# The last head's values ahead of the fourth modulation in a decode block: the order of one load and of the matmuls behind it

## The chip, the cores and the metric

The kernel runs on one core of a Trainium2 chip. The metric is the device time of one execution in microseconds (us); the median of three runs stands for a kernel. The profile is of one execution of its own, and its times are counted from the start of its span.

## What is computed

A transformer block in decode: two sequences (B = 2), one new token each, model width 512, 32 heads of width 128 over 4096 cached positions, everything in 32-bit floats. Conditioning vectors `c` give six modulations (shift, scale and gate of each half). Cut to its core, the reference is:

```
mod = silu(c) @ w_mod                    # [2, 6 * 512] -> sa, ca, ga, sb, cb, gb  (modulations 0 to 5)
h = layernorm(x) * (1 + ca) + sa
q = h @ wq                               # 32 heads x 128
p = softmax(q . k_cache * 128**-0.5)     # over 4096 positions, per head
x = x + ga * ((p @ v_cache) @ wo)        # ga: modulation 2
h = layernorm(x) * (1 + cb) + sb         # cb: modulation 4, sb: modulation 3
h = h @ w1 + b1                          # 512 -> 1376
x = x + gb * ((h * tanh(softplus(h))) @ w2)   # gb: modulation 5
```

The two caches alone are 268 MB, and each value of them is used once.

## The kernel before, in words

**Loads.** The host lays all inputs out beforehand as one stream of rows of 128 partitions. `stream()` (lines 40 to 75) lists 36 loads in order. Most fill one buffer of 64 KB a partition; there are three such buffers (tile name `room`), so load n can be issued only when the readers of load n-3 in the same place are done (`used`, line 167). `load` (line 146) issues a load's transfers from SyncE (SP), line 163, in the order of the list. In the trace all of them are "room<-in_load", L163.

The last four loads (lines 66 to 74) matter here. Load 32 has the values of head 28, the last two pieces of `wo` and modulation 2. Load 33 has the values of heads 29 and 30. Load 34 (line 69) has the weights of modulation 4 (`m4`, 1024 KB) and the values of head 31, in two parts of 2048 KB (`("v", 31, 0)` and `("v", 31, 1)`); it goes as a transfer of 3072 KB (`m4` and part 0) and two of 1024 KB (the halves of part 1). Behind them in the same load stands `m5p`, a part of modulation 5's weights that uses only 24 rows. It goes in eight small transfers over rows named in `DEAL` (line 18): three of one row, two of three rows, three of five rows, 8 KB a row. `EARLY = 4` (line 17) says how many of the eight are issued ahead of the load's large transfers; the rest come behind them (lines 160 to 163). Load 35 has modulation 3 with half of `w1` (2400 KB), the other half (1376 KB), then the rest of modulation 5 with the first chunk of `w2` (1024 KB), and the other ten chunks of `w2` in four transfers (1280, 768, 256 and 256 KB).

**Heads.** For each head, VectorE multiplies the keys by the query (line 342) and sums (line 345), 8.7 us each; this runs beside the stream. TensorE (PE) weights the values (`weighted_v`, line 379, matmul at line 385) into a PSUM bank.

**Tail.** The order of all instructions is written out by hand. From line 484 on, PE does: values of heads 29 and 30 with a stretch of `busy` dummies between; `head_values` and `project_o` for them; part 0 of head 31's values (line 521); `fold_att` (line 522, matmul at 516), which folds the attention output of the other heads; part 1 of head 31's values (line 523), in the middle of which, through the argument `idle`, stand three quarters of modulation 4 (`modulation`, matmul at line 271). Then the sums of head 31 are copied out (line 524), turned (line 526, matmul at 408) and projected (`head_out_q`, line 528, matmul at 424); the last quarter of modulation 4 follows (line 529), two dummies, and two terms of modulation 5 (line 548, matmul at 543). VectorE makes the new x (lines 552 and 555); `centred` (line 224) takes its mean and variance by two small matmuls (lines 234 and 242), and what stands in its argument `between` is issued to PE in the middle: here three dummies (line 559). Then come modulation 3 (line 560), two more terms of modulation 5, the first feed-forward matmul (line 577), the activation, the rest of modulation 5, the second feed-forward matmul over eleven chunks of `w2` (line 622), and two VectorE operations (629, 630) before the store.

`busy(n)` (line 318, matmul at 322) issues matmuls whose result nobody reads, one instruction of the program for up to two blocks of 128 columns. A 32-bit matmul shows as two instructions in the trace, so `busy(3)` is four of them and `modulation` over three quarters is 24.

Of the kernel before, what the change touches and what calls it, by code (L numbers as in the profile page):

```python
# [9 lines left out]
AF = mybir.ActivationFunctionType  # L10
# [3 lines left out]
P = 128  # L14
WIDTHS = (384, 384, 352, 256)
CHUNKS = [(g, j) for j in range(3) for g in range(4) if WIDTHS[g] > P * j]
EARLY = 4
DEAL = [slice(j, j + 1) for j in (33, 34, 35)] + [slice(32, 41, 4), slice(3, 12, 4)] + [slice(j, 20, 4) for j in range(3)]
PLACES = sorted(p for deal in DEAL for p in range(deal.start, deal.stop, deal.step or 1))
BLOCK = 44  # L20
# [1 line left out]
WHOLE = len(PIECES)  # L22
# [6 lines left out]
W = 2048  # L29
HALF = BIG // 2  # L30
# [9 lines left out]
def stream():  # L40


    order, n_v = [], 0
    for h in range(1, HEADS):
        order.append(("k", h))
        if h % HC == HC - 1 and HC < h < HEADS - 1:
            c = (h + 1) // HC
            order.append([("wq", c), ("wo", c - 2)])
        if h not in AHEAD:
            order += [("v", n_v, 0), ("v", n_v, 1)]  # L50
            n_v += 1
    order = [x if isinstance(x, list) else [x] for x in order]

    def size(x):
        return sum(SIZES[key[0]] for key in x)

    loads = [[([("m01", 0), ("wq", 0), ("wq", 1)], (4 * W,)), ([("k", 0)], (BIG,))]]
    for _ in range(1, HEADS):
        row = []
        while size(row) < ROW:  # L60
            room = ROW - size(row)
            row += order.pop(next(i for i, x in enumerate(order) if size(x) <= room))
        loads.append([(row, (ROW,))])
    last = [("v", h, i) for h in range(HEADS - 4, HEADS) for i in range(2)]
    assert order == [[key] for key in last[:2]], order
    loads += [
        [(last[:2] + [("wo", 6), ("wo", 7), ("m2", 0)], (BIG + 3 * W,))],
        [(last[2:4], (BIG,)), (last[4:6], (BIG,))],
        [([("m4", 0)] + last[6:], (W + HALF, W, W)), ([("m5p", 0)], (512 * WHOLE,))],
        [  # L70
            ([("m3", 0), ("w1", 0)], (W + 2 * sum(WIDTHS), 2 * sum(WIDTHS))),
            ([("m5", 0), ("w2", 0)], (512 * (M5 + 1), 5 * 512, 3 * 512, 512, 512)),
        ],
    ]
    return loads
# [3 lines left out]
def kernel(  # L79
# [17 lines left out]
    nc = tc.nc  # L97
# [7 lines left out]
    H = HEADS  # L105
# [13 lines left out]
    def small_ps(name):  # L119
        return psum.tile([P, 512], F32, tag="sm", name=name, bufs=2)  # L120

    def wide_ps(name):
        return psum.tile([P, 512], F32, tag="mm", name=name, bufs=2)
# [19 lines left out]
    w_t = {}  # L143
    done = set()

    def load(n):
# [3 lines left out]
        for keys, srcs in loads[n]:  # L150
            take(t[:, lo:], keys)
            for src in srcs:
# [5 lines left out]
                else:  # L158
                    nc.gpsimd.memset(dst, 0.0)  # L159
                    deals = [(dst[deal], src[deal]) for deal in DEAL]  # L160
                    early, parts = deals[:EARLY], parts + deals[EARLY:]
        for dst, src in early + parts:
# [4 lines left out]
    def used(*keys):  # L167

        nonlocal loaded
        done.update(keys)  # L170
        while loaded < len(loads) and (
            loaded < 3 or all(key in done for keys, _ in loads[loaded - 3] for key in keys)
        ):
            load(loaded)
            loaded += 1
# [8 lines left out]
    bias = const.tile([P, NJ * G + NP5 * B], F32, name="bias")  # L184
    nc.scalar.dma_start(out=bias, in_=b1c)
    c5 = bias[:, NJ * G :]
    bias = bias[:, : NJ * G]
# [36 lines left out]
    def centred(src, name, first_sum=None, between=None):  # L224

        rs = const.tile([P, 8], F32, name=f"rs_{name}")
        xc = work.tile([P, P], F32, tag="xc", name=f"xc_{name}", bufs=1)
        sq = work.tile([P, P], F32, tag="sq", name=f"sq_{name}", bufs=1)
        if first_sum is None:
            nc.vector.tensor_reduce(out=rs[:, 0:1], in_=src, axis=AX.X, op=ALU.add)  # L230
        else:
            first_sum(rs[:, 0:1])
        mps = small_ps(f"mean_{name}")
        nc.tensor.matmul(mps[:, 0:1], lhsT=mean_w, rhs=rs[:, 0:1], start=True, stop=True)
        nc.vector.tensor_scalar(out=xc, in0=src, scalar1=mps[:, 0:1], scalar2=None, op0=ALU.subtract)
        nc.vector.scalar_tensor_tensor(
            sq, xc, 1.0, xc, op0=ALU.mult, op1=ALU.mult, accum_out=rs[:, 1:2]
        )
        if between is not None:
            between()  # L240
        vps = small_ps(f"var_{name}")
        nc.tensor.matmul(vps[:, 0:1], lhsT=mean_w, rhs=rs[:, 1:2], start=True, stop=True)
        return xc, vps[:, 0:1], rs
# [20 lines left out]
    def modulation(name, n, t, ps=None, ks=range(G)):  # L264


        if ps is None:
            ps = wide_ps(f"modps{name}")[:, : n * P].rearrange("p (m n) -> p m n", m=n)
        for k in ks:
            for g in range(G):  # L270
                nc.tensor.matmul(  # L271
                    ps[R * g : R * (g + 1)],
                    lhsT=ct[:, k, :],
                    rhs=t[:, k, :].rearrange("p (m n) -> p m n", m=n)[:, :, P * g : P * (g + 1)],
                    start=(k == 0),
                    stop=(k == G - 1),
                )
        return ps
# [9 lines left out]
    xc, var, rs = centred(xq, "a")  # L288
# [29 lines left out]
    def busy(n, bank=1):  # L318

        for lo in range(0, n, 2):  # L320
            cols = P * min(2, n - lo)
            nc.tensor.matmul(ov[bank][:, :cols], lhsT=ident, rhs=e_t[0].rearrange("p c m -> p (c m)")[:, :cols], start=True, stop=True)  # L322


    NB = NS // 4
# [50 lines left out]
            out=t[:, :4, :], in0=own, in1=t[:, 4:5, :].to_broadcast([P, 4, B * HC]), op=ALU.mult,  # L376
        )

    def weighted_v(h, part, bank, first=True, last=True, idle={}):

        for c in range(NB // 2):
            if c in idle:
                idle[c]()
            g = c % G
            nc.tensor.matmul(  # L385
                ov[bank][R * g : R * (g + 1), :],
                lhsT=e_t[h % HC][:, NB // 2 * part + c, :],
                rhs=v_t[h, part][:, c, :],
                start=(first and part == 0 and c < G),
                stop=(last and part == 1 and c >= NB // 2 - G),  # L390
            )
        used(("v", h, part))

    def value_sums(bank, copies):

        o_t.clear()
        n = 4 // len(copies)
        for i, copy in enumerate(copies):
            o = work.tile([P, 4, DH], F32, tag="o", name=f"o{bank}")[:, :n]
            copy(o.rearrange("p m d -> p (m d)"), ov[bank][:, n * DH * i : n * DH * (i + 1)])  # L400
            for m in range(n):
                o_t[n * i + m] = o[:, m, :]
# [18 lines left out]
    def head_out_q(h):  # L421

        for g in range(G):
            nc.tensor.matmul(
                xps[R * g : R * (g + 1), :P],
                lhsT=ot_t[h // HC % 2][:, h % HC, :],
                rhs=wo_t[h // HC][:, h % HC, P * g : P * (g + 1)],
                start=False, stop=(h == H - 1), skip_group_check=True,
            )
# [54 lines left out]
    N = H // HC - 1  # L484
# [13 lines left out]
    for h in range(H - 3, H - 1):  # L498
        if h == H - 2:
            busy(24, 1 - N % 2)  # L500
        for part in range(2):
            weighted_v(h, part, N % 2, False, h == H - 2)
# [8 lines left out]
    mps4 = wide_ps("modps4")[:, :P].rearrange("p (m n) -> p m n", m=1)  # L511

    def fold_att():

        for g in range(G):
            nc.tensor.matmul(
                xps[R * g : R * (g + 1), :P], lhsT=fold, rhs=att_sb[:, P * g : P * (g + 1)],
                start=True, stop=False, skip_group_check=True,
            )

    weighted_v(H - 1, 0, 1 - N % 2)
    fold_att()
    weighted_v(H - 1, 1, 1 - N % 2, idle={NB // 4: lambda: modulation("4", 1, w_t["m4"], mps4, (0, 1, 2))})
    value_sums(1 - N % 2, (nc.scalar.copy, nc.vector.tensor_copy))
    busy(3)
    head_values(N, HC - 1, HC)
    busy(2)
    head_out_q(H - 1)
    modulation("4", 1, w_t["m4"], mps4, (3,))
    busy(2)  # L530
    wm3, wm5 = w_t["m3"], w_t["m5"]
    w1_t, w2_t = w_t["w1"], w_t["w2"]
    gps = ov[1 - N % 2][:, :P]
# [5 lines left out]
    def modulation_5(lo, hi):  # L539
        for n in range(lo, hi):  # L540
            c, w = terms5[n]
            for g in range(G):
                nc.tensor.matmul(  # L543
                    gps[R * g : R * (g + 1)], lhsT=c, rhs=w[:, P * g : P * (g + 1)],
                    start=(n == 0), stop=(n == len(terms5) - 1),
                )

    modulation_5(0, 2)

    xg = work.tile([P, P], F32, tag="sq", name="xg", bufs=1)  # L550
    x2 = const.tile([P, P], F32, name="x2")
    nc.vector.tensor_tensor(out=xg, in0=xps[:, :P], in1=mod[2], op=ALU.mult)
# [2 lines left out]
        nc.vector.scalar_tensor_tensor(x2, xg, 1.0, xq, op0=ALU.mult, op1=ALU.add, accum_out=total)  # L555

    m4 = work.tile([P, P], F32, tag="xn", name="m4", bufs=1)
    nc.scalar.activation(m4, mps4[:, 0, :], AF.Copy, bias=1.0)
    xc, var, rs = centred(x2, "b", add_x, lambda: busy(3))
    mps3 = modulation("3", 1, wm3)  # L560
    busy(1)
    modulation_5(2, 4)
# [156 lines left out]
```

## Time and profile before

| what | us |
|---|---|
| median of 3 runs (lowest, highest) | 694.71 (694.52, 694.92) |
| the profiled execution's own time | 694.6 |
| its span | 693.2 |
| VectorE busy, share of the span | 587.9, 85% |
| PE busy | 289.9, 42% |
| data moved, mean rate | 297.48 MB, 429 GB/s |

The span runs from the first to the last instruction of the program; 1.4 us of the execution's own time lie around it. In a row of the timeline stand the start, the time from the first start to the last end, engine, line, operation, tiles (out<-in), shapes and count, and in brackets how long the engine had been idle and what ended that. PE is a matmul, PEld the weight load ahead of it. In a row of the table by stretches stand the stretch, its length, each engine's busy time with its instructions, the clock granted to PE (1.00 is full), the busy share of the sixteen DMA engines (it can pass 1 by rounding at the edges) and GB/s.

### The profile page before, as it was taken

Reading aid. Unit: us, or ns where it says so; the run is one execution under the profiler, and the core shown is the slowest. Engines: PE = TensorE matmul, PEld = TensorE weight load, DVE = VectorE, ACT = ScalarE, POOL = GpSimd, SP = SyncE. Lnnn points to the kernel's source line nnn. Section 1 sums busy time; section 2 is a strip of 40 time slices with the busy share of each in tenths; the row PEclk is TensorE's granted clock in tenths of the full one; section 3 lists DMA queues with packets and bytes.
Section 4 is the critical chain, followed back from the end, with each engine's and each line's share of the span. In section 5 each row is a group of like instructions: output and inputs, shape, how many; then the busy total and the mean of one; then the engine's idle time right before and its main releaser. Section 6 shows DMA issues by size and latency. Waiting matters only on the chain.

```text
span 693.2 us, 4056 instructions
## 1 busy us (share of the span) xinstructions
PE 289.9 (42%) x1698; PEld 109.5 (16%) x1698; DVE 587.9 (85%) x223; ACT 44.2 (6%) x169; POOL 6.3 (1%) x21
## 2 busy tenths in 40 slices
PE   3403334335145524335242716245334425134898
PEld 1201001001012201101100301011101111001355
DVE  2799899999999999999999999999999999899202
ACT  1000000000000000000000000000000010000011
POOL 2000000000000000000000000000000000000100
PEclk9855666668565566556585565656575657656799
DMA  9999999999999999999999999999999999999997
GB/s 381 467 424 424 425 424 469 429 427 431 424 425 465 428 427 436 424 431 451 427 427 442 425 450 431 427 428 442 424 446 429 424 446 432 427 439 419 423 429 318
DMA packets 6994, 297.48 MB, mean 429 GB/s; under 512 B 928, under 2 KB 1064, under 8 KB 1448
## 3 DMA queue, kind: packets, MB, share of 16 engines
q1 hardware_dynamic: 6672, 297.14, 99.2%
q8 instruction: 13, 0.21, 0.1%
q10 hardware_dynamic: 304, 0.09, 0.1%
q14 instruction: 5, 0.04, 0.0%
HBM read 297.16 MB, written 0.07 MB: 429 GB/s over the span
## 4 chain that ended last, share of the span: by engine, by line
DMA 68%; DVE 28%; PE 4%; issue 0%; ACT 0%; SPq 0%; DVEq 0%; ACTq 0%
DMA room<-in_load 68%; DVE room L342 14%; DVE s L345 14%; PE modps L271 1%; PE ov L322 1%; PE qps L315 1%; PE w1ps L577 0%; PE yps L622 0%; PE ov L543 0%; PE ov L385 0%; PE fps L592 0%; PE otp L408 0%; DVE m L358 0%; DVE hcw L304 0%; ACT q L316 0%
## 5 line engine op out<-in xcount | busy, mean ns | idle before, releaser
L342 DVE TENSOR_TENSOR room<-room,q 128x8192 f32<-128x8192 f32 x32 | 278.2, 8693 | 45.3 <-DMA room<-in_load 40.9
L345 DVE TENSOR_REDUCE s<-room 128x64 f32<-128x8192 f32 x32 | 277.9, 8684 | 0.4 <-DVE m L358 0.3
L385 PE MATMUL ov<-room,e 128*32 128x512 f32 x1024 | 174.0, 834 | 73.1 <-ACT e L361 63.2
L354 PE MATMUL mt<-d,same 128*128 128x64 f32 x64 | 18.6, 385 | 196.4 <-DVE d L352 196.4
L385 PEld LDWEIGHTS ov<-room,e 128*32 128x32 f32 x1024 | 39.0, 145 | 177.6 <-issue 130.7
L361 ACT ACTIVATE e<-s,m 64x64 f32<-64x64 f32 x64 | 22.1, 345 | 554.2 <-DVE m L358 553.4
L354 PEld LDWEIGHTS mt<-d,same 128*128 128x128 f32 x64 | 13.4, 262 | 226.4 <-DVE d L352 180.9
L315 PE MATMUL qps<-room,hcw 128*128 128x512 f32 x64 | 42.0, 819 | 4.2 <-DMA room<-in_load 3.5
L369 PE MATMUL l<-l,ones 128*128 128x8 f32 x16 | 4.6, 359 | 74.9 <-ACT e L361 74.9
L408 PE MATMUL otp<-pick,o 128*128 128x8 f32 (+2 forms) x72 | 14.3, 326 | 34.5 <-ACT o L400 32.6
L315 PEld LDWEIGHTS qps<-room,hcw 128*128 128x128 f32 x64 | 16.4, 268 | 25.1 <-issue 19.7
L408 PEld LDWEIGHTS otp<-pick,o 128*128 128x128 f32 x72 | 13.6, 282 | 42.6 <-ACT o L400 39.8
L400 DVE COPY o<-ov 128x256 f32<-128x256 f32 x1 | 0.4, 425 | 22.9 <-ACT o L400 22.9
L369 PEld LDWEIGHTS l<-l,ones 128*128 128x128 f32 x16 | 3.8, 297 | 76.3 <-ACT e L361 76.3
L416 PE MATMUL att<-room,ot 128*32 128x512 f32 x62 | 10.2, 718 | 5.2 <-DMA room<-in_load 4.6
L361 ACT ACTIVATION_READ_ACCUMULATOR e<-s,m 64x1 f32 x64 | 11.8, 184 | 0.0
L322 PE MATMUL ov<-e,ident 128*128 128x256 f32 (+1 forms) x46 | 11.4, 380 | 0.0
L358 DVE TENSOR_REDUCE m<-mt 128x1 f32<-128x64 f32 x32 | 7.0, 218 | 5.1 <-PE mt L354 5.1
L352 DVE TENSOR_SCALAR d<-half,m 128x64 f32<-128x64 f32 x32 | 9.6, 299 | 1.1
L322 PEld LDWEIGHTS ov<-e,ident 128*128 128x128 f32 x46 | 8.0, 190 | 3.8 <-issue 3.1
L350 DVE TENSOR_REDUCE m<-s 128x1 f32<-128x64 f32 x32 | 7.0, 218 | 0.9
L159 POOL MEMSET room<- 44x2048 f32 x1 | 1.8, 1804 | 637.2 <-DVE s L345 637.2
(108 smaller groups left out, 71.4 us busy)
## 6 DMA issues: line engine op xcount, KB each, us to landing
room<-in_load SPq DMA_DIRECT2D x4, 4096.0 KB, 25.0
room<-in_load SPq DMA_DIRECT2D x1, 7168.0 KB, 38.9
room<-in_load SPq DMA_DIRECT2D x1, 3072.0 KB, 22.4
room<-in_load SPq DMA_DIRECT2D x3, 1024.0 KB, 22.0
room<-in_load SPq DMA_DIRECT2D x1, 2400.0 KB
room<-in_load SPq DMA_DIRECT2D x1, 1376.0 KB, 14.0
room<-in_load SPq DMA_DIRECT2D x1, 1280.0 KB, 14.4
room<-in_load SPq DMA_DIRECT2D x1, 768.0 KB
```

The costliest lines, as they stand in the source:

```text
L315: nc.tensor.matmul(ps, lhsT=hcw[:, k, :], rhs=wq_t[ch][:, k, :], start=(k == 0), stop=(k == G - 1))
L322: nc.tensor.matmul(ov[bank][:, :cols], lhsT=ident, rhs=e_t[0].rearrange("p c m -> p (c m)")[:, :cols], start=True, stop=True)
L342: nc.vector.tensor_tensor(out=k_t[h], in0=k_t[h], in1=qv, op=ALU.mult)
L345: nc.vector.tensor_reduce(out=s_t[h], in_=k_t[h], axis=AX.X, op=ALU.add)
L350: nc.vector.tensor_reduce(out=m_t[h][:, 0:1], in_=s_t[h], axis=AX.X, op=ALU.max)
L352: nc.vector.tensor_scalar(out=d, in0=half, scalar1=m_t[h][:, 0:1], scalar2=None, op0=ALU.mult)
L354: nc.tensor.matmul(mps[h], lhsT=same, rhs=d, start=True, stop=True)
L361: nc.scalar.activation(e_t[i][own_b, :, M * i + 4 * b : M * i + 4 * b + 4], s_t[h][own_b].rearrange("p (c m) -> p c m", m=4), AF.Exp, bias ...
L369: nc.tensor.matmul(lps[n], lhsT=ones, rhs=sum_t[n % 2], start=True, stop=True)
L385: nc.tensor.matmul(ov[bank][R * g : R * (g + 1), :], lhsT=e_t[h % HC][:, NB // 2 * part + c, :], rhs=v_t[h, part][:, c, :], start=(first a ...
L408: nc.tensor.matmul(tps[:, x], lhsT=o_t[m], rhs=pick_t[n][:, m, x], start=(m == 0), stop=(m == 3),)
L416: nc.tensor.matmul(att[R * i : R * (i + 1), :], lhsT=ot_t[n % 2][:, i, :], rhs=wo_t[n][:, i, :], start=(n == 0), stop=(n == H // HC - (2 i ...
```

## The change

In load 34 the values of head 31 stand first and modulation 4 behind them: the transfers are now 2048 KB (part 0), 1024 and 1024 KB (part 1) and 1024 KB (`m4`), one more than before. Five of the eight small transfers of `m5p` go ahead instead of four, the fifth being one of three rows. On PE, three quarters of modulation 4 move from the middle of head 31's values to behind `head_out_q`. Its last quarter, the copy of its result on ScalarE, and the first two terms of modulation 5 move into the middle of `centred`, in place of the three dummies; two more dummies are gone. The argument `idle` goes, as nothing uses it.

```diff
@@ -14,7 +14,7 @@
 P = 128
 WIDTHS = (384, 384, 352, 256)
 CHUNKS = [(g, j) for j in range(3) for g in range(4) if WIDTHS[g] > P * j]
-EARLY = 4
+EARLY = 5
 DEAL = [slice(j, j + 1) for j in (33, 34, 35)] + [slice(32, 41, 4), slice(3, 12, 4)] + [slice(j, 20, 4) for j in range(3)]
 PLACES = sorted(p for deal in DEAL for p in range(deal.start, deal.stop, deal.step or 1))
 BLOCK = 44
@@ -66,7 +66,7 @@
     loads += [
         [(last[:2] + [("wo", 6), ("wo", 7), ("m2", 0)], (BIG + 3 * W,))],
         [(last[2:4], (BIG,)), (last[4:6], (BIG,))],
-        [([("m4", 0)] + last[6:], (W + HALF, W, W)), ([("m5p", 0)], (512 * WHOLE,))],
+        [(last[6:] + [("m4", 0)], (HALF, W, W, W)), ([("m5p", 0)], (512 * WHOLE,))],
         [
             ([("m3", 0), ("w1", 0)], (W + 2 * sum(WIDTHS), 2 * sum(WIDTHS))),
             ([("m5", 0), ("w2", 0)], (512 * (M5 + 1), 5 * 512, 3 * 512, 512, 512)),
@@ -376,11 +376,9 @@
             out=t[:, :4, :], in0=own, in1=t[:, 4:5, :].to_broadcast([P, 4, B * HC]), op=ALU.mult,
         )
 
-    def weighted_v(h, part, bank, first=True, last=True, idle={}):
+    def weighted_v(h, part, bank, first=True, last=True):
 
         for c in range(NB // 2):
-            if c in idle:
-                idle[c]()
             g = c % G
             nc.tensor.matmul(
                 ov[bank][R * g : R * (g + 1), :],
@@ -520,14 +518,13 @@
 
     weighted_v(H - 1, 0, 1 - N % 2)
     fold_att()
-    weighted_v(H - 1, 1, 1 - N % 2, idle={NB // 4: lambda: modulation("4", 1, w_t["m4"], mps4, (0, 1, 2))})
+    weighted_v(H - 1, 1, 1 - N % 2)
     value_sums(1 - N % 2, (nc.scalar.copy, nc.vector.tensor_copy))
     busy(3)
     head_values(N, HC - 1, HC)
     busy(2)
     head_out_q(H - 1)
-    modulation("4", 1, w_t["m4"], mps4, (3,))
-    busy(2)
+    modulation("4", 1, w_t["m4"], mps4, (0, 1, 2))
     wm3, wm5 = w_t["m3"], w_t["m5"]
     w1_t, w2_t = w_t["w1"], w_t["w2"]
     gps = ov[1 - N % 2][:, :P]
@@ -545,8 +542,6 @@
                     start=(n == 0), stop=(n == len(terms5) - 1),
                 )
 
-    modulation_5(0, 2)
-
     xg = work.tile([P, P], F32, tag="sq", name="xg", bufs=1)
     x2 = const.tile([P, P], F32, name="x2")
     nc.vector.tensor_tensor(out=xg, in0=xps[:, :P], in1=mod[2], op=ALU.mult)
@@ -555,8 +550,14 @@
         nc.vector.scalar_tensor_tensor(x2, xg, 1.0, xq, op0=ALU.mult, op1=ALU.add, accum_out=total)
 
     m4 = work.tile([P, P], F32, tag="xn", name="m4", bufs=1)
-    nc.scalar.activation(m4, mps4[:, 0, :], AF.Copy, bias=1.0)
-    xc, var, rs = centred(x2, "b", add_x, lambda: busy(3))
+
+    def between():
+
+        modulation("4", 1, w_t["m4"], mps4, (3,))
+        nc.scalar.activation(m4, mps4[:, 0, :], AF.Copy, bias=1.0)
+        modulation_5(0, 2)
+
+    xc, var, rs = centred(x2, "b", add_x, between)
     mps3 = modulation("3", 1, wm3)
     busy(1)
     modulation_5(2, 4)
```

## Prediction

> **What bounds the kernel now.** I read the page first, then the table by stretches for the end of the stream, then the timeline of the last 30 us, then the issues of the late loads.
>
> ```profile
> span 693.2 us, 4056 instructions
> q1 hardware_dynamic: 6672, 297.14, 99.2%
> ```
>
> The load queue kept the sixteen DMA engines busy for 99.2% of the span: the kernel lasts as long as its stream, plus what is left after it. How much is left, by stretches of the end:
>
> ```profile
> 674.00:684.00 10.00, 9.95 (x136) 7.49 (x139) 2.86 (x13) 1.68 (x6) 0.42 (x1) 1.00 0.99 418
> 684.00:687.00 3.00, 2.44 (x40) 1.62 (x36) 0.18 (x1) 0.78 (x4) 0.00 (x0) 1.00 1.00 419
> 687.00:688.00 1.00, 1.00 (x25) 0.52 (x14) 0.84 (x5) 0.03 (x1) 0.00 (x0) 1.00 0.82 334
> 688.00:689.00 1.00, 1.00 (x30) 0.75 (x32) 0.29 (x2) 0.00 (x0) 0.00 (x0) 1.00 0.69 270
> 689.00:690.00 1.00, 1.00 (x46) 1.00 (x40) 0.00 (x0) 0.00 (x0) 0.00 (x0) 1.00 0.47 162
> 690.00:691.00 1.00, 0.87 (x32) 0.58 (x24) 0.07 (x1) 0.00 (x0) 0.00 (x0) 1.00 0.00 0
> ```
>
> The last number but one is the DMA share: full to 687, then some engines run dry, and the last bytes move at about 690.0. That is late: the second feed-forward matmul, which ends the kernel, has been running since 688.25. So two ends are close together, the stream's and that of the tail's own chain. The timeline of the tail shows the second:
>
> ```profile
> 667.84 1.25 PEld L385 LDWEIGHTS ov<-room,e 128*32 128x32 f32 x16 [0.47 <-DMA room<-in_load]
> 669.60 0.61 PE L516 MATMUL xps<-att_sb,fold 128*32 128x128 f32 x8
> 670.26 0.16 PEld L385 LDWEIGHTS ov<-room,e 128*32 128x32 f32 x8 [0.32 <-DMA room<-in_load]
> 671.15 0.84 PE L271 MATMUL modps<-room,ct 128*32 128x128 f32 x24
> 672.88 0.16 PEld L385 LDWEIGHTS ov<-room,e 128*32 128x32 f32 x8 [1.16 <-DMA room<-in_load]
> 673.88 0.92 PE L322 MATMUL ov<-e,ident 128*128 128x256 f32 x4
> 676.05 0.43 PE L424 MATMUL xps<-room,ot 128*32 128x128 f32 x8
> 676.30 0.40 PE L271 MATMUL modps<-room,ct 128*32 128x128 f32 x8
> 676.63 0.70 PE L322 MATMUL ov<-e,ident 128*128 128x256 f32 x2
> 677.09 0.08 DVE L555 DVE_READ_ACCUMULATOR x<-xg,cx 128x1 f32 x1
> 677.26 0.64 PE L543 MATMUL ov<-room,ct 44*32 44x128 f32 x16
> 677.83 0.38 PE L234 MATMUL mean_b<-rs_b,mean_w 128*128 128x1 f32 x2
> 678.07 0.90 PE L322 MATMUL ov<-e,ident 128*128 128x256 f32 x4
> 678.79 0.08 DVE L236 DVE_READ_ACCUMULATOR sq_b<-xc_b 128x1 f32 x1
> 679.02 0.35 PE L242 MATMUL var_b<-rs_b,mean_w 128*128 128x1 f32 x2
> 679.31 1.08 PE L271 MATMUL modps<-room,ct 128*32 128x128 f32 x32
> 682.38 2.77 PE L577 MATMUL w1ps<-room,h2t 128*32 128x384 f32 x32
> 688.25 2.61 PE L622 MATMUL yps<-room,actt 96*32 96x128 f32 x88
> 690.93 0.29 DVE L629 TENSOR_TENSOR y<-yps,mod 128x128 f32<-128x128 f32 x1 [2.64 <-PE yps L622]
> ```
>
> Three times PE waits for head 31's values: the transfer of 3072 KB is there at 667.84, the next two of 1024 KB at 670.26 and 672.88. From there to 690.93 the chain of waits names no DMA.
>
> **The change part by part.** The landing times of all that follows are needed. Two issues of load 35 show theirs, the second half of `w1` and the five chunks of `w2`:
>
> ```profile
> L163 SPq DMA_DIRECT2D room<-in_load x1: 328/328/328, 667.8 to 667.8; - x1
> DMA to landing us min/median/max: 14.0/14.0/14.0
> ...
> L163 SPq DMA_DIRECT2D room<-in_load x1: 328/328/328, 672.9 to 672.9; - x1
> DMA to landing us min/median/max: 14.4/14.4/14.4
> ```
>
> So the second half of `w1` is complete at 667.8 + 14.0 = 681.8 and the five chunks at 672.9 + 14.4 = 687.3. The pace in between is that of the slowest engines: 670.26 - 667.84 = 2.42 us for 1024 KB. Between 672.84 and 681.8 lie 2400 + 1376 KB, 9.0 us, the same pace. Modulation 3 with the first half of `w1` therefore lands at about 672.84 + 9.0 x 2400/3776 = 678.5. After 687.3 come 768, 256 and 256 KB, at that pace 1.8, 0.6 and 0.6 us: landings at about 689.1, 689.7 and 690.3. These are estimates, and the last agrees with bytes that move until 690.0.
>
> *Order of the load.* The bytes stay the same. Part 0 now comes 1024 KB earlier (667.84 - 2.42 = 665.4), the last quarter of the values takes the middle slot (670.26), and `m4` the last (672.88). The fifth early transfer puts at most three rows of 8 KB (24 KB) ahead of the values; spread over its engines that is one row each, 8/64 of a 1024 KB transfer's share of an engine (64 KB), 2.42/8 = 0.3 us, and only if it hit a slowest engine. All from load 35 on keeps its place in the stream.
>
> *One transfer more, in SP's queue.* A late issue of load 35 comes at the landing of an earlier transfer (672.9 against the landing that PE saw at 672.88; 667.8 against 667.84), so issues are held by earlier landings. With one transfer more, and smaller ones, these come no later than before. A late issue would be covered by the 14 us of stream queued ahead of it; with that cover gone each microsecond would move the end. The stream itself pays for the cut of rows of 24 KB into 16 and 8 KB. Bounds: nothing, as 3072 + 1024 KB in long rows should do no better than the 2.42 us per 1024 KB seen for 8 KB rows; and 0.2 us, as the second such transfer took 672.88 - 670.26 = 2.62. A gain is excluded, since no bytes go. I take 0.05, nearer the first pair. The Trainium skill ("DMA: Bandwidth & Descriptors", Anatomy of one DMA) gives each transfer a fixed 2.0 us besides its bytes, on the GpSimd path; by that a queued transfer more would cost 2.0. The measured 2.42 us for a whole queued transfer speaks against it here.
>
> *PE up to the projection.* Part 0 of head 31 no longer waits, and starts at 667.84 or up to 0.2 before, when the work ahead of it ends. From its start to the fold are 669.60 - 667.84 = 1.76 us, the fold takes about 0.4 (0.66 to the next start less most of the 0.32 waited), part 1 another 1.76, with no wait since its last quarter is there at 670.26. The dummies then start at 671.8 instead of 673.88: 2.1 earlier, not 2.6, since PE's work is now the limit. The projection (676.05) moves to 674.0.
>
> *Modulation 4 and the dummies.* Three quarters of it, 24 matmuls of 0.84 us together, lay in the wait for the values and now stand behind the projection. There they run while VectorE makes x (676.05 to 677.17, 1.1 us), which covers them; with no cover they would cost 0.84. `m4` is there at 672.9, 1.1 before. What they replace was longer: last quarter 0.33 (676.30 to 676.63), dummies 0.63, modulation 5 0.57, which held the mean's matmul until 677.83 though x was summed at 677.17. The mean now starts at about 675.1, 2.7 earlier. In the middle of the mean and the variance, 0.33 + 0.57 = 0.9 of real work replaces three dummies of about 0.9. The variance comes at about 676.25, 2.8 earlier.
>
> *What is late next.* Modulation 3's matmuls could start at 676.5, and their weights land at 678.5. So 2.0 of the 2.8 us turn into a wait, with the rest of PE's queue behind it: this stage starts 0.8 before its old 679.31. The same 0.8 carries to the second feed-forward matmul, at 687.5. It takes (2.61 - 0.27)/87 x 8 = 0.215 us a chunk (0.27 is the drain of one matmul). Chunk 6 is wanted at 687.5 + 6 x 0.215 = 688.8 and lands at 689.1; the last chunk is then wanted at 690.0 and lands at 690.3. Before, it was wanted at 688.25 + 10 x 0.215 = 690.4. So the end moves by -0.1 for the wait that ends last, +0.05 for the cut rows: about nothing. On the profiled execution's 694.6 that is 694.55; the median stands 0.1 above it, at 694.71, so I say 694.6 for the median. Of 2.8 us made in the middle all are lost again to the weights behind.
>
> **The rivals.** *The stream does not bind at the end* (faster). If the estimated landings were wrong and all 2.8 us reached the end, the time would be 691.9. For it: the chain of waits names PE, not DMA, after 672.88. Against it: bytes move until 690.0, so the last chunk can't be worked on before; even with landings at the last bytes the gain is 0.4. Chance 0.02.
>
> *The clock falls in the new wait* (slower). PE idles from 676.6 to 678.5, where the dummies kept it busy. Earlier in the trace such gaps set the clock of the next 3.41 us:
>
> ```profile
> 586.85:590.27 3.42, 1.43 (x16) 0.22 (x8) 3.42 (x1) 0.00 (x0) 0.00 (x0) 1.00 1.04 446
> 590.27:593.68 3.41, 0.00 (x0) 0.00 (x0) 3.41 (x3) 0.14 (x1) 0.00 (x0) 1.00 0.97 423
> 648.29:651.71 3.42, 1.64 (x16) 0.88 (x16) 1.11 (x6) 1.35 (x6) 0.00 (x0) 1.00 0.99 419
> 651.71:655.12 3.41, 3.41 (x20) 0.85 (x16) 0.00 (x0) 0.00 (x0) 0.00 (x0) 0.50 0.92 396
> ```
>
> A stretch with PE busy 1.64 of 3.42 (0.48) was followed by the half clock, one with 1.43 (0.42) was not: somewhere under a half it decides. A stretch that holds the whole gap of 1.9 has 1.5 busy (0.44), one that cuts the gap has more. A half clock for 3.41 us loses up to 1.7 of PE work, less the 0.8 in hand: the end 0.9 later, 695.5, still within 0.2%. Two such stretches lose 3.4, less 0.8: 697.2, slower. For the second, the half-clock stretch would have to be idle too; modulation 3 and `w1` fill it, and a full one (651.71) went back to 1.00 at once. Chance of one 0.15, of two 0.04. The Trainium skill ("TensorE: Matmul & The Clock Gate", Part 1) drops the clock only after about 3.4 us of idling; by that this gap costs nothing and the time is the forecast's. The stretch of 0.48 shows that less can do.
>
> *A transfer more is paid in the stream* (slower). The upper bound is what a whole transfer of 1024 KB takes, 2.42 us: 697.0; it decides once the price passes 1.4 us. Against it the pace above, where one follows on the other with nothing between. Chance 0.02. By the fixed time in the Trainium skill ("DMA: Bandwidth & Descriptors", Anatomy of one DMA) it would be 696.6.
>
> **How the numbers follow.** Forecast (nothing reaches the end) 0.77, clock once 0.15, clock twice 0.04, a paid transfer 0.02, a free tail 0.02. A measurement of this kernel tells about 0.2%, 1.4 us, from no change. Faster 0.02; slower 0.06; the same 0.92. The range takes the forecast with the last bytes' 0.4 below, 694.3, to the one fall of the clock, 695.6.
>
> **What would show it.** In the changed profile: head 31's three value groups at L385 without a DMA wait, the dummies after them at about 671.8; the projection (L424) at 674.0, the mean (L234) at 675.1; a wait of about 2 us for a load ahead of L271 x32, which starts at 678.5; the start of L622 at 687.5 with its 88 matmuls stretched to about 3.2 us; the last bytes at 690.0 as before, y (L629) within 0.2 of 690.93. The forecast is wrong if the DMA share falls to zero well before or after 690.0, or if the granted clock shows 0.5 after 676.

## The result and the profile after

| kernel | median us (lowest, highest, executions) | span of the profiled execution |
|---|---|---|
| before | 694.80 (694.52, 695.17, 6) | 693.2 |
| after | 698.38 (697.50, 698.94, 6) | 696.8 |

The ratio is 1.005, with a 95% interval of 1.004 to 1.006: slower by 3.6 us, where no change was forecast. First the page of the changed kernel, its span and its load queue:

```profile
span 696.8 us, 4044 instructions
q1 hardware_dynamic: 6816, 297.14, 98.7%
```

The stream did not become longer: 98.7% of 696.8 is 687.7 us of packets, and of before 99.2% of 693.2 was 687.7. Nor does it end later. By stretches (the last number but two is the clock granted to PE, the last but one the DMA share):

```profile
688.00:689.00 1.00, 0.81 (x9) 0.11 (x2) 0.00 (x0) 0.05 (x1) 0.00 (x0) 1.00 0.68 270
689.00:690.00 1.00, 0.62 (x6) 0.63 (x6) 0.00 (x0) 0.53 (x3) 0.00 (x0) 1.00 0.42 162
690.00:691.00 1.00, 1.00 (x30) 0.78 (x34) 0.43 (x3) 0.22 (x1) 0.00 (x0) 1.00 0.02 6
```

The shares are 0.68, 0.42 and 0.02, against 0.69, 0.47 and 0.00 of before. The loss lies in the tail's own chain. The timeline of it, rows that answer to those of before:

```profile
670.41 0.16 PEld L383 LDWEIGHTS ov<-room,e 128*32 128x32 f32 x8 [1.10 <-DMA room<-in_load]
671.40 0.92 PE L322 MATMUL ov<-e,ident 128*128 128x256 f32 x4
673.58 0.43 PE L422 MATMUL xps<-room,ot 128*32 128x128 f32 x8
674.76 0.38 PE L234 MATMUL mean_b<-rs_b,mean_w 128*128 128x1 f32 x2
676.00 0.38 PE L242 MATMUL var_b<-rs_b,mean_w 128*128 128x1 f32 x2
678.73 1.93 PE L271 MATMUL modps<-room,ct 128*32 128x128 f32 x32 [2.35 <-DMA room<-in_load]
682.33 0.59 PE L261 MATMUL h2ps<-ident,hq 128*128 128x8 f32 x2
684.33 4.48 PE L578 MATMUL w1ps<-room,h2t 128*32 128x384 f32 x32
689.38 0.83 PE L593 MATMUL fps<-ident,hq_pad 128*128 128x8 f32 x6 [0.56 <-ACT hq_pad L590]
691.92 2.61 PE L623 MATMUL yps<-room,actt 96*32 96x128 f32 x88
694.59 0.29 DVE L630 TENSOR_TENSOR y<-yps,mod 128x128 f32<-128x128 f32 x1 [2.63 <-PE yps L623]
```

Up to the variance all is early, by 679.02 - 676.00 = 3.0 us. Modulation 3 then waits 2.35 us for its weights, takes 1.93 us instead of 1.08, and the first feed-forward matmul 4.48 instead of 2.77. The second starts at 691.92, 3.67 later than before (688.25), and y is 694.59 - 690.93 = 3.66 later. The stretches of the clock show why:

```profile
674.16:677.57 3.41, 2.12 (x48) 1.36 (x39) 1.92 (x10) 1.14 (x4) 0.00 (x0) 1.00 0.99 425
677.57:680.98 3.41, 2.25 (x34) 1.77 (x34) 0.19 (x1) 0.00 (x0) 0.00 (x0) 0.50 0.96 408
680.98:684.40 3.42, 3.42 (x28) 2.37 (x31) 0.33 (x2) 0.00 (x0) 0.00 (x0) 0.50 1.04 432
684.40:687.81 3.41, 3.41 (x26) 2.09 (x29) 0.00 (x0) 0.00 (x0) 0.00 (x0) 0.50 0.94 393
687.81:691.22 3.41, 2.85 (x48) 1.72 (x41) 0.61 (x4) 0.81 (x4) 0.00 (x0) 1.00 0.38 150
```

In the wait the clock falls to 0.50 and stays there for three stretches, 10.2 us. In the kernel before, the tail runs at 1.00 throughout.

### The profile page after: what moved, and what is told of

Read it like the earlier page. It is cut to its first block, busy times and chain, and to the rows that moved or that the text cites. A ratio compares the mean times of both kernels' runs of the same rounds, so it can differ in the third digit from the quotient of the medians.

```text
span 696.8 us, 4044 instructions
## 1 busy us (share of the span) xinstructions
PE 291.4 (42%) x1692; PEld 110.9 (16%) x1692; DVE 589.8 (85%) x223; ACT 44.2 (6%) x169; POOL 6.2 (1%) x21
## 3 DMA queue, kind: packets, MB, share of 16 engines
q1 hardware_dynamic: 6816, 297.14, 98.7%
## 4 chain that ended last, share of the span: by engine, by line
DMA 67%; DVE 28%; PE 4%; issue 0%; ACT 0%; SPq 0%; DVEq 0%; ACTq 0%
DMA room<-in_load 67%; DVE room L342 14%; DVE s L345 14%; PE modps L271 1%; PE qps L315 1%; PE w1ps L578 1%; PE ov L383 1%; PE ov L322 0%; PE yps L623 0%; PE ov L540 0%; PE fps L593 0%; DVE m L358 0%; DVE hcw L304 0%; ACT q L316 0%; PE hps L261 0%
## 5 line engine op out<-in xcount | busy, mean ns | idle before, releaser
L383 PE MATMUL ov<-room,e 128*32 128x512 f32 x1024 | 170.0, 814 | 67.8 <-ACT e L361 49.7
L315 PE MATMUL qps<-room,hcw 128*128 128x512 f32 x64 | 46.2, 891 | 4.7 <-DMA room<-in_load 3.9
L315 PEld LDWEIGHTS qps<-room,hcw 128*128 128x128 f32 x64 | 17.9, 292 | 27.7 <-issue 21.9
L414 PE MATMUL att<-room,ot 128*32 128x512 f32 x62 | 10.2, 719 | 5.2 <-DMA room<-in_load 4.6
L271 PE MATMUL modps<-room,ct 128*32 128x128 f32 (+1 forms) x128 | 7.9, 400 | 3.6 <-DMA room<-in_load 3.6
```

The source lines that it names most:

```text
L271: nc.tensor.matmul(ps[R * g : R * (g + 1)], lhsT=ct[:, k, :], rhs=t[:, k, :].rearrange("p (m n) -> p m n", m=n)[:, :, P * g : P * (g + 1)] ...
L315: nc.tensor.matmul(ps, lhsT=hcw[:, k, :], rhs=wq_t[ch][:, k, :], start=(k == 0), stop=(k == G - 1))
L383: nc.tensor.matmul(ov[bank][R * g : R * (g + 1), :], lhsT=e_t[h % HC][:, NB // 2 * part + c, :], rhs=v_t[h, part][:, c, :], start=(first a ...
L414: nc.tensor.matmul(att[R * i : R * (i + 1), :], lhsT=ot_t[n % 2][:, i, :], rhs=wo_t[n][:, i, :], start=(n == 0), stop=(n == H // HC - (2 i ...
```

## The experiments

Theory A: the gap ahead of modulation 3 takes the clock, and the stage behind it can't win it back soon. Theory B: the loss comes from the loads themselves. Theory C: the dummies that went were needed.

**The gap filled with nine dummies** (`fill9`).

```diff
+    busy(9)
     mps3 = modulation("3", 1, wm3)
```

> The changed kernel with nine dummies more (five instructions of the program, about 2.0 us) between the variance's matmul and modulation 3, where PE idled for 2.35 us. Theory A (the loss is the half clock that this gap brings, which the stage behind it can't leave for three stretches of 3.41 us): the granted clock stays at 1.00 from 647 on, modulation 3 still starts at 678.7 when its weights land, L623 starts at about 687.7 instead of 691.9, and the time is 694.6 to 694.9, bounded by the last chunk of w2. Theory B (the loss lies in the loads: one transfer more, or weights that come late in the stream): 698.4 as the change.

Measured: 694.78 us in 11 executions (694.51 to 695.28), ratio to before 1.000 (0.9991 to 1.0008). The loads are the changed ones, so theory B falls. The timeline:

```profile
678.47 1.08 PE L271 MATMUL modps<-room,ct 128*32 128x128 f32 x32
680.47 0.39 PE L261 MATMUL h2ps<-ident,hq 128*128 128x8 f32 x2
681.54 2.77 PE L579 MATMUL w1ps<-room,h2t 128*32 128x384 f32 x32
684.87 0.84 PE L594 MATMUL fps<-ident,hq_pad 128*128 128x8 f32 x6 [0.56 <-ACT hq_pad L591]
...
687.42 1.52 PE L624 MATMUL yps<-room,actt 96*32 96x128 f32 x48
689.09 1.08 PE L624 MATMUL yps<-room,actt 128*32 128x128 f32 x32 [0.15 <-DMA room<-in_load]
690.34 0.43 PE L624 MATMUL yps<-room,actt 128*32 128x128 f32 x8 [0.17 <-DMA room<-in_load]
```

The clock holds in the stretch with the dummies and in the one after it:

```profile
676.65:680.06 3.41, 3.30 (x51) 2.61 (x54) 0.86 (x4) 0.58 (x2) 0.00 (x0) 1.00 0.99 418
680.06:683.48 3.42, 3.42 (x49) 2.53 (x44) 0.17 (x1) 0.00 (x0) 0.00 (x0) 1.00 1.01 422
```

Here is the forecast's own course: modulation 3 at 678.5, the second feed-forward matmul at 687.4, and there it waits twice for `w2`, the last chunk at 690.34. The run also gives the bill of the half clock. From modulation 3 to that matmul are 687.42 - 678.47 = 8.95 us here and 691.92 - 678.73 = 13.19 in the change, 4.24 more. Of these, 1.6 come up to the turning matmul (3.60 against 2.00), 0.9 up to the first feed-forward matmul (2.00 against 1.07) and 1.7 in it (5.05 against 3.33); the rest runs equally fast.

**Real work in the gap** (`fill_work`).

```diff
+    modulation_5(2, 4)
+    busy(6)
     mps3 = modulation("3", 1, wm3)
-    busy(1)
-    modulation_5(2, 4)
```

> The changed kernel with work in the gap: two terms of modulation 5 (0.6 us) come ahead of modulation 3 instead of behind it, with six dummies (1.4 us) after them, and the one dummy behind modulation 3 goes. Theory A: clock 1.00 to the end; L271 x32 at 678.6, h2ps about 0.8 earlier than with nine dummies, the second feed-forward matmul starting at about 686.7; but the last chunk of w2 lands at 690.3 to 690.5 as ever, so 694.6 to 694.8: what is won in the middle is lost at the end. If the stream didn't bind there, 693.9.

Measured: 694.71 us (694.53 to 695.05, 11 executions), ratio 1.000 (0.9991 to 1.0008).

```profile
687.35 1.52 PE L623 MATMUL yps<-room,actt 96*32 96x128 f32 x48
689.34 1.08 PE L623 MATMUL yps<-room,actt 128*32 128x128 f32 x32 [0.46 <-DMA room<-in_load]
690.58 0.43 PE L623 MATMUL yps<-room,actt 128*32 128x128 f32 x8 [0.16 <-DMA room<-in_load]
```

The clock held (1.00 from 675.80 to 679.22, the stretch with the gap, and in the whole tail after it). The matmul starts at 687.35 rather than the 686.7 expected, and still waits for the same chunks. With this stream its end is bound by the last chunk, so a still earlier start would gain nothing. No version of this study beats the kernel before.

**Three dummies in the gap** (`fill3`): `busy(3)` at the same place.

> The changed kernel with three dummies (about 0.7 us) in the gap ahead of modulation 3 instead of nine; about 1.6 us of idling stays. Theory A with a bound on how much of a stretch of 3.41 us PE may be without work: the clock holds in some executions or in all, depending on where the stretches fall, so a time between 694.7 and 698.4, with single runs near either end. If only a gap as long as a stretch counted, 694.7 throughout.

Measured: median 695.05, ratio 1.0024 (1.0010 to 1.0039), and in the single executions two groups: seven of twelve from 694.54 to 695.13, four from 698.50 to 698.82, one at 696.94. By their times, the same program either keeps the clock or pays the change's price; a profile is kept of one execution alone, and that one kept the clock, with 1.44 us of waiting ahead of modulation 3:

```profile
676.25:679.67 3.42, 1.98 (x38) 1.54 (x39) 0.53 (x3) 0.86 (x3) 0.00 (x0) 1.00 0.95 405
679.67:683.08 3.41, 3.41 (x46) 2.54 (x50) 0.52 (x2) 0.00 (x0) 0.00 (x0) 1.00 1.02 429
```

**The order on PE alone** (`pe_only`): the changed kernel with `EARLY = 4` and `m4` ahead of the values in its load.

```diff
-EARLY = 5
+EARLY = 4
-        [(last[6:] + [("m4", 0)], (HALF, W, W, W)), ([("m5p", 0)], (512 * WHOLE,))],
+        [([("m4", 0)] + last[6:], (W + HALF, W, W)), ([("m5p", 0)], (512 * WHOLE,))],
```

> The loads of before (modulation 4 ahead of the values, EARLY = 4) with the order of PE of the change, so also without its dummies. Head 31's last values come at 672.9, the variance at about 678.6, modulation 3's weights at 678.5: no gap is left. Theory A: clock 1.00 to the end, 694.6. Theory B: 694.6 too, as the loads are those of before. Theory C (the dummies that went were needed to hold the clock): the clock falls after 676, 697 to 698.5.

Measured: 694.68 us (694.42 to 695.13, 11 executions), ratio 0.9998 (0.9990 to 1.0007).

```profile
678.34 0.38 PE L242 MATMUL var_b<-rs_b,mean_w 128*128 128x1 f32 x2
678.65 1.08 PE L271 MATMUL modps<-room,ct 128*32 128x128 f32 x32
```

```profile
674.32:677.73 3.41, 3.32 (x55) 2.54 (x53) 1.23 (x5) 0.16 (x1) 0.42 (x1) 1.00 0.98 421
677.73:681.14 3.41, 3.41 (x75) 2.65 (x72) 1.62 (x9) 1.14 (x4) 0.00 (x0) 1.00 1.00 424
```

With the values later the variance comes at 678.34, just ahead of the weights: no gap, no fall, although the dummies are gone here too. By the busy time the moved work takes their place.

**The loads alone** (`loads_only`): the kernel before with `EARLY = 5` and `m4` behind the values.

```diff
-EARLY = 4
+EARLY = 5
-        [([("m4", 0)] + last[6:], (W + HALF, W, W)), ([("m5p", 0)], (512 * WHOLE,))],
+        [(last[6:] + [("m4", 0)], (HALF, W, W, W)), ([("m5p", 0)], (512 * WHOLE,))],
```

> The loads of the change with the order of PE of before. Three quarters of modulation 4 stand in the middle of head 31's values and now wait for weights that land at 672.9, with the last eight value matmuls behind them: those start at about 673.6, 0.7 later than before. Theory A: with a clock that holds, 695.3; the wait of about 1.9 us ahead of modulation 4 follows on a stretch full of values, so the share need not fall below the bound. If it does fall, 697 or more. Theory B: 698.4.

Measured: median 696.92, ratio 1.0051 (1.0021 to 1.0081), in three groups of single executions: four from 695.41 to 695.52 (near the 695.3 expected if the clock holds, the 0.7 us of the later values; none of these four was profiled, so that is not shown), five from 696.79 to 697.07, three from 704.42 to 704.78. The profile caught one of the last; a wait of 2.74 us ahead of modulation 4 stands in the first of these stretches:

```profile
670.73:674.14 3.41, 1.05 (x28) 0.81 (x32) 0.00 (x0) 0.00 (x0) 0.00 (x0) 1.00 1.06 449
674.14:677.55 3.41, 3.41 (x17) 2.11 (x9) 0.42 (x1) 0.37 (x1) 0.00 (x0) 0.50 0.97 415
677.55:680.97 3.42, 3.42 (x24) 2.30 (x24) 0.59 (x3) 0.44 (x2) 0.42 (x1) 0.50 0.98 416
680.97:684.38 3.41, 3.41 (x24) 2.21 (x23) 0.80 (x4) 0.00 (x0) 0.00 (x0) 0.50 1.01 426
684.38:687.79 3.41, 3.41 (x46) 2.67 (x48) 0.88 (x4) 0.86 (x3) 0.00 (x0) 0.50 0.98 408
687.79:691.21 3.42, 3.42 (x30) 2.36 (x25) 0.17 (x1) 0.00 (x0) 0.00 (x0) 0.50 0.40 155
691.21:694.62 3.41, 3.41 (x29) 1.97 (x22) 0.00 (x0) 0.00 (x0) 0.00 (x0) 0.50 0.00 0
```

PE is busy in the whole of every stretch after the first, and the clock stays at half for six of them.

**The dummies alone** (`no_dummies`): the kernel before without them.

```diff
     modulation("4", 1, w_t["m4"], mps4, (3,))
-    busy(2)
...
-    xc, var, rs = centred(x2, "b", add_x, lambda: busy(3))
+    xc, var, rs = centred(x2, "b", add_x, None)
```

> The kernel before without the two dummies behind modulation 4 and the three in the middle of mean and variance; nothing else changed. Theory A: about 1.0 us less of dummies but no gap over 1 us; the clock holds and the weights bound the end: 694.6. Theory C (the dummies that went were needed): the clock falls after 676, 697 to 698.5.

Measured: median 697.25, ratio 1.0032 (1.0023 to 1.0041); nine of eleven executions from 697.15 to 698.67, two at 694.50 and 695.59. Theory A's number was a miss: the clock falls here with no long gap, the longest wait of PE in the stretch that lost it being 0.81 us (ahead of the variance's matmul).

```profile
675.54:678.96 3.42, 2.61 (x47) 1.78 (x51) 1.39 (x7) 0.53 (x3) 0.20 (x1) 1.00 0.98 416
678.96:682.37 3.41, 3.41 (x51) 2.38 (x43) 0.88 (x4) 0.77 (x3) 0.00 (x0) 0.50 1.02 429
```

So theory C holds for the kernel before: its dummies are needed. For the change it does not suffice, as `pe_only` lacks them too and keeps the clock. Both fit one cause in two forms, too little work for PE in a stretch; how much is too little is the subject of the next section.

**More work after the gap** (`dense`): `busy(8)` right behind modulation 3 of the changed kernel.

> The changed kernel with eight dummies of 256 columns right behind modulation 3, after the gap, in the stage that runs at half clock. Theory A, with recovery hanging on how densely columns are streamed and not on the busy time that the profile shows: the clock falls as in the change but comes back one stretch earlier, after two (6.8 us) instead of three. The time: eight dummies cost up to 3.6 us at half clock, one stretch less gives back up to 1.7: 699 to 701. If density does not matter the clock stays down for three stretches or more: 701 to 702.

Measured: 697.31 us (695.71 to 697.43, 4 executions), ratio 1.0033 (1.0020 to 1.0045). Work that nobody reads, put on the path, made the changed kernel 1.1 us faster by the medians, outside what was expected: the half clock lasted one stretch, not two.

```profile
675.27:678.69 3.42, 1.89 (x40) 1.21 (x36) 1.65 (x9) 1.14 (x4) 0.00 (x0) 1.00 0.97 412
678.69:682.10 3.41, 3.41 (x36) 2.71 (x37) 0.35 (x1) 0.00 (x0) 0.00 (x0) 0.50 0.99 421
682.10:685.51 3.41, 3.41 (x38) 2.68 (x40) 0.17 (x1) 0.00 (x0) 0.00 (x0) 1.00 1.01 422
```

**Four early transfers** (`early4`): the changed kernel with `EARLY = 4`; then once more beside the changed kernel itself.

> The changed kernel with EARLY = 4, so four small transfers ahead of the values as before; all else as changed. Theory A: the gap is the same, the values at most 0.3 us earlier, the clock falls: 698 (697.5 to 699). If the fifth early transfer is to blame: 694.7.

> The changed kernel with EARLY = 4 once more, beside the changed kernel itself on the same chip. If the fifth early transfer lengthens the fall of the clock by one stretch: 697.2 in nearly all executions again. If where the stretches of 3.41 us fall decides, by chance from execution to execution: a spread over 697 to 699, the same as the changed kernel's.

> The changed kernel unaltered, beside the one with EARLY = 4. If the fifth early transfer matters: 698.4 in nearly all executions. If the place of the stretches decides: a spread over 697 to 699 like the other's.

Measured: 697.20 (697.15 to 697.56, 4 executions), then 697.22 (696.91 to 697.45, 6), beside 698.49 (697.86 to 698.89, 5) for the change. The fall is there without the fifth early transfer, so that is not its cause; but it is shorter by one stretch, 6.8 us instead of 10.2:

```profile
676.73:680.15 3.42, 1.56 (x38) 1.24 (x42) 0.88 (x4) 0.62 (x3) 0.00 (x0) 1.00 0.97 414
680.15:683.56 3.41, 3.41 (x27) 2.37 (x27) 0.17 (x2) 0.00 (x0) 0.00 (x0) 0.50 1.01 422
683.56:686.97 3.41, 3.41 (x29) 2.15 (x24) 0.00 (x0) 0.00 (x0) 0.00 (x0) 0.50 0.99 414
```

The stretches end at 676.7 and 680.1 here, in the change at 674.2 and 677.6, so modulation 3, from 678.59, still runs at full clock (1.08 us). Why 24 KB in another place should shift that in all ten executions is not settled.

## Why the prediction was wrong

*What held.* The stream and its end: the last bytes move at 690.0 and in `fill9` and `fill_work`, where the clock holds, the last chunk is worked on from 690.34 and 690.58 on. One transfer more cost nothing that shows in the stream (687.7 us of packets both times), so the 2.0 us of the Trainium skill ("DMA: Bandwidth & Descriptors", Anatomy of one DMA) were not paid here. The sums up to the variance: dummies at 671.4 (671.8 forecast), projection 673.6 (674.0), mean 674.8 (675.1), variance 676.0 (676.25), each a little early. Head 31's first values start at 666.41, within the project matmuls ahead of them, and not at 667.84 as in the sum. So PE reaches the last quarter of the values before it has landed: the weight load at 670.41 had waited 1.10 us for it, though the prediction named no such wait and took PE's own work for the limit. That is a second miss, of 0.4 us, and it does not reach the end. The wait ahead of modulation 3: 2.35 us where about 2 were forecast, until 678.73 where 678.5 was.

*What failed.* The rival named "the clock falls in the new wait" is what happened: all eleven executions of the change took 697.50 us or more. Its chance (0.15 for one stretch, 0.04 for two) was too low and its price too small. Two steps did it.

First, "somewhere under a half it decides", from two rows of busy time. The busy time of the profile is no measure for this. The stretch that lost the clock in the change was busy for 2.12 of 3.41 us, 0.62, where the prediction reckoned with 0.44. A stretch with 1.98 of 3.42 (`fill3`) kept the clock, one with 2.61 of 3.42 (`no_dummies`) lost it.

Counting columns does better. In this estimate a matmul counts for the time in which its columns stream: 128 columns take 0.107 us at full clock (half of the 0.215 us a chunk in the prediction, as a chunk is two groups of four matmuls) and twice that at half clock. The four matmuls of a group run side by side and count once. A one-column matmul counts as nothing, though the profile gives it 0.38 us a pair. The prediction's own two rows come to 0.27 of the stretch for the one that lost the clock (from 648.29) and 0.37 for the one that kept it (from 586.85): the busy time, 0.48 and 0.42, has them the wrong way round. In the change's stretch from 674.16 there remain about 0.6 us of modulation 4 and 0.5 of modulation 5: 1.06 of 3.41, or 0.31. Around the gap the same count gives 0.45 for `no_dummies`, 0.37 for `early4` and 0.24 for `dense`, all of which fell, and 0.47 for `fill3`, 0.52 for `pe_only` and 0.65 or more for `fill9`, which held. It does not yet order all: stretches made mostly of value matmuls held at 0.37 and 0.43 in `pe_only`, while `no_dummies` fell at 0.45 and the change's second profile at 0.44.

These last two hold the terms of modulation 5 that use 44 of the 128 rows. If every matmul is counted at its share of the 128 rows, both come to 0.35, and narrow bounds do come out over the whole stretches of the twelve kept traces between 30 and 692 us. At full clock all 352 stretches under 0.36 were followed by the half clock and all 348 of 0.40 or more by the full one; of the 37 in between 5 fell. At half clock all 1193 under 0.72 stayed there and all 348 of 0.80 or more went back; of the 38 in between 18 stayed. The weighting by rows was chosen after the fact, for those two stretches, and no run isolates it.

Second, the price: one stretch of half clock, 1.7 us less the 0.8 in hand, because "a full one (651.71) went back to 1.00 at once". That stretch was full of value matmuls of 512 columns, 0.98 by the count. The stage behind the gap has short matmuls and hands its results to VectorE and back. Its first stretch at half clock still holds 1.16 us of the wait and is busy for 2.25 of 3.41; it comes to 0.57 by the count of columns. The second, although 3.42 of 3.42 busy by the profile, comes to 0.72, or 0.55 with the rows counted too. The clock came back after the third, which `w1` filled (1.0). By the count without the rows, in `loads_only` five stretches of 0.63 to 0.77 stayed at half and one of 1.0 went back; in `dense` one of 0.9 was enough. With three stretches instead of one the loss between modulation 3 and the second feed-forward matmul is 4.24 us; less the 0.6 that the stage started early (679.31 - 678.73; 0.8 in the prediction) that is the 3.67 measured at L623. `fill9` differs from the change by work in the gap alone and takes all of it away: that the gap cost the 3.6 us, through the clock, is shown. The bounds are read off the traces by an estimate; which property of a matmul counts is not shown.

The rule of the Trainium skill ("TensorE: Matmul & The Clock Gate", Part 1) was read as no fall under 3.4 us of idling. The trace differs: the clock fell after 677.57 - 676.38 = 1.2 us of idling within a stretch that the profile shows 62% busy, and a stretch shown as busy throughout did not bring it back. Its free-running window of 3.41 us agrees with the rows: in the change's two profiles the clock falls at the end of such a stretch, at 677.57 and at 677.04.

## To carry to other kernels

Where one part of a chain is made earlier, look for the next load it needs: the time turns into an idle wait there, and on PE an idle wait has a price of its own. Before dummy matmuls are taken away or displaced, count what is left for PE in each stretch of 3.4 us by columns streamed, not by the profile's busy time: in these traces, with the rows counted too, 0.4 of a stretch kept the full clock, and 0.8 of one won it back. Judge a wait also by what follows: ahead of a stage of short, dependent matmuls a fall of the clock lasted three stretches here, and with eight dummies more in that stage (`dense`) one.

## What the runs showed of the hardware beyond that

Single executions of one program fall into groups (694.5 to 695.1 and 698.5 to 698.8 in `fill3`; 695.4, 696.8 to 697.1 and 704.4 to 704.8 in `loads_only`). In the profiled executions the time goes with how long the clock fell: 694.86 us with no fall (`fill3`), 697.15 and 697.20 with two stretches (`early4`, `no_dummies`), 698.37 with three (the change), 704.78 with six (`loads_only`). `dense` took 697.26 with one stretch and eight dummies on its path. That the other executions of a group fell alike is taken from their times. A median or one profile alone does not tell such a kernel's time. The spread is then part of the result: 0.8 us from lowest to highest for `fill9`, 9.4 us for `loads_only`.
